# DeltaNet and an MLP mixer in one kernel: 54 steps take another place in the order of issue

## The chip, the cores and the metric

The kernel runs on one core of a Trainium2 chip. A core has a matrix engine (TensorE, PE in the profile, with its weight loads as PEld), a vector engine (DVE), a scalar engine (ACT), GpSimd (POOL) and a queue that issues the transfers between DRAM and on-chip memory (SyncE, SP). Each engine works through its own instructions in the order in which the program issued them, and waits at an instruction until the data and buffers that it needs are there. The metric is the device time of one execution in microseconds (us).

## The reference

Two blocks in a row, all in float32. The first is a DeltaNet attention over 4 batches, 8 heads, 768 positions and a head width of 48:

```
k_n = k / (norm(k) + 1e-6)
for t in range(768):                       # per batch and head
    y[t]  = q[t] @ state                   # state is 48 x 48, from zero
    v_old = state^T k_n[t]
    state = state + beta[t] * outer(k_n[t], v[t] - v_old)
```

The second takes y as x (4 x 768 x 384) and is an MLP mixer, first over tokens, then over channels:

```
h  = relu(x^T @ w_tok1) @ w_tok2           # 768 -> 256 -> 768
u  = x + h^T
out = u + relu(u @ w_ch1) @ w_ch2          # 384 -> 1536 -> 384
```

## The kernel before

**DeltaNet in chunks.** The 768 positions are cut into chunks of 64. Inside a chunk the recurrence is written as matrix products with the inverse of a triangular 64x64 matrix, so that only the step from chunk to chunk is serial. Chunks are handled in units of two (u = 0 to 23). The work on a unit is cut into jobs: `k` loads keys and queries, `p` normalizes and transposes them, `c` (and `d`) make the Gram products, `t` writes the triangular matrices to DRAM (n_dram), `i` inverts a round of several units at once on DVE (x is loaded from n_dram, eliminated row by row on lines 747 and 751, and stored to w_dram), `f` loads the inverses (gm from w_dram), `j` joins parts of an inverse to the whole (p_z and p_x on PE, copies to zst and gm on ACT), `v` loads the values and scales them on POOL. `r0` to `r35` are the serial recurrences. `r24` to `r35` (`recur_pair`) walk through two batches at once: steps 1 to 4 are the p_k products on PE (L1013), step 5 is rw_t on DVE (L1022), steps 6 and 7 are p_y and p_w on PE (L1038, L1042), step 8 is the copy of rw_t on ACT (L1047), steps 9 and 10 are p_s and p_y on PE (L1056, L1059), step 11 updates the state ss_t on DVE (L1070), steps 12 and 13 are ACT's copies of y (L1076, L1081), and step 14 stores one of them to x_dram. The last, `r35`, has no update: its steps 11 to 13 are the two copies and the store.

**The mixer.** `m0` and `m1` (`mixer`) do batches 0 and 1: first the token part (p_h, L1612, with an add of DVE on L1616), then products of the channel part over pieces of 128 rows (p_c, L1672, p_o, L1693) with sums on DVE (L1652) and adds on DVE (L1632). `T2` (`token_part`) is the token part of batch 2: steps 1 to 6 are four matmuls each (L1227), steps 7 to 12 are p_h (L1242) with an add (L1246). `T3`, `S`, `s`, `W` and `A`, `F`, `B` are the token part of batch 3, sums and forms of the weights, and the channel part of batches 2 and 3; `l` loads batch 3 from x_dram.

**The order.** Each job is a Python generator that issues a few instructions between two `yield`s. One long string, written out by hand, names the job whose next step is issued: `m1*4 i4` is four steps of m1 and one of i4. It has 2610 steps.

```python
    for word in order.split():
        name, _, n = word.partition("*")
        for _ in range(int(n or 1)):
            next(jobs[name])
```

The string is the only thing that sets who stands in front of whom on each engine. All transfers are issued on SP. Buffers come from pools that rotate: PSUM, where products land, is divided by tags into 2 buffers for the preparation of units, 2 for the recurrences (`ps_seq`), 3 for the mixer (`ps_mlp`, which the recurrences of pairs borrow from) and one more; a product waits until the reader of what was in its buffer before is done. A transfer also waits for the one eight before it.

Of the kernel before, what the change touches and what calls it, by code (L numbers as in the profile page):

```python
# [23 lines left out]
def kernel(  # L24
# [1756 lines left out]
    w10 p0*2 z w3 w2 c0*3 p0 w3*2 d0*2 w3 c0 p1 c0 d0*3 k2*3 v1 p1*2 w18 k2*2 p1*2  # L1781
    c1*2 d1 k2 p2*2 c1 t0 d1 c1*2 d1*3 t0 p2*8 c2*2 w2 d2 c2*3 Y d2 w2 k3*6 p3
    d2*2 p3 d2 t1*3 x p3*7 c3 k4*5 k7 w13 w18*2 d3*2 v1*2 v0*2 c3*3 v0 c3 d3*3 t0
    p4*2 t2*3 x t3*2 p4*2 x t3 i0*2 w13 p4*2 w18 w17*2 i0 k4 i0*9 p4 i0*2 p4*2 c4
    k8 c4*3 w13*2 w6*2 k5*2 v0 k6 k5*2 i0*2 d4*2 k5 x z d4*3 c4 z*2 p5*2 k5 t4 p5
    h0 h1 h0 w8*2 h1 Y i0 f0 Y p4 f1 h2*2 p5*3 f0*2 w6 h0*5 k6*5 p6 z f2*2 k8*3 p5
    w6 p5 p3 p5 j0*3 f1*2 h1*5 j0*2 w8*2 w17 f2 h2*3 v0 t4*2 w17 r0*5 p6 h2*2 c5*2
    v1 w11*2 j1 p5 k7*2 c5 k7 c5 r0 c5 r0*2 w14*2 v1 w11*2 k7*2 p7 d5*5 r1*5 w14*2
    p6*2 t5 j1 t5*2 r1*2 j1 j2 p7 h3*2 r1*3 p6*3 i1*2 r2*5 k8*2 f3*2 w9 k9*3 j1*2
    v2*2 i1*3 j2*2 r2*2 f3 i1*2 p6*3 w16 v2 w16*3 r2*2 h3 r2 i1 d6 r3*5 i1*2 w9*3  # L1790
    v2 d6 h3 v2 w0 h3*2 r3 h3 d6*2 w0 d6 j3 c6*5 r3*4 w0 j2 w0 p8*2 j2 r4 p8 r4*4
    k9*3 j3*2 r4*2 i1*2 w24 i1*2 p7*7 r4 c7 r4 r5*5 k10 p9 k10 p9 c7 r4 c7*3 i1
    w5*2 p7 r5*2 w24*3 r5*3 j3*2 i1 r6*4 w26 v3*5 p9 k11 r6 d7*5 w26*3 p8*3 t6*2
    r6*2 w5*2 p8*4 v4*2 t6 i1 r6*3 h5*2 h4*2 k10*2 f4*3 c8*2 k10 p10 w28*2 c8*2 r7
    c8 r7*3 d8*4 p9 d8 w28 h4*5 p9 t6 r7*2 j4 w28 p9*3 r7*2 p9 w7 d9 w7 v4*2 f5*2
    w27*2 w7*2 d9*4 c9*2 f5 c9*3 t7*2 t8 r7*2 t7*2 j4*2 v4 p10*2 h5 r8*3 w29 t8*3
    w29 w27*2 r8*2 w29*2 q3 w29 j4*2 r8 w22*4 t9*3 r8*3 p9 r9 p10 r9*3 t9 v5 h5*3
    j5 i2 r9 w4*2 r8 h5 i2*5 w4 i2 w19*2 k10 w32 p10*2 w32 v7 k12 m0*2 k11 k12 q0
    v5*3 p10*2 r9*2 j5*2 k11*3 i2*2 r9 w4 i2 j5 i2*3 p10 v5 r9*2 d10*3 r10 v7*2 j5
    i2*2 r10*4 w12 i2 k12 i2*2 m0 w32 k11 k12 w32 r10*2 m0 p11 k12*4 w19 p11 r10  # L1800
    c10 r10 c10 r10 w33 d10*2 q2 Y r11*4 v7 r11*3 w19 c10 q1 w30 c10 r11 k12*2
    i2*3 r11 v6*4 i2*5 m0*3 i2*5 q5 i2 m0 p11*4 c10 p11 m0 p11*2 m0*2 k12*2 w12
    m0*3 v6 f6*3 w12 d11 c11*2 d11*2 c11 w33 c11 d11*2 j6 p12 w12 m0 w33 w30*3
    p12*2 f7*3 j6*2 m0 c11 j7 f6 f8 w27*2 f8 j7 f8 w15 f7 m0 w29 w33 w29 j7 r12*4
    w31 j8 p11 t10*3 r12 Y r12 f9 j8 f9 w21 p12 r12 f8 r13*2 w15*2 r12 w15 r13*3
    w31*3 Y r13*2 w33 j8 w21 m0 r13 q4 p12*4 r13*2 m0*2 r14 c12 f9 j9 r14*2 w21
    t10 w20*2 v7 r14*2 c12*2 w33 c12 r14 v8 c12*2 r14*2 w25*2 j9 r14 r15 v8 w21
    r14 r15 w25 r15*3 w25 k13*4 w20 k13*4 p13 k13*2 w20 v8*3 m0*2 p13 w25 p13 m0
    r15 p13 r15 p13 w27 w25 k13*2 j9 m0*4 p13 f9 w23 t12*3 p13 t12 w25 r15*3 c13*6
    w23 k14*7 r16*5 m0 p13 m0*3 w23*4 k14 r16*2 t11 t13*2 j9*2 t11*3 w33 p14 r16*2  # L1810
    p14*2 w31 m0*3 w31 m0 w31 m0 w23 r17*2 r16 t13 r17 t13 r17*2 p14*2 m0*2 p14 i3
    k14*4 i3*3 k15 v9*2 m0*3 v10 i3*5 k15 i3 r17 k15*2 p14 k15*3 m0 v10*2 i3 k15*2
    m0*2 k15*2 i3*4 r17*4 k15 i3*2 p14 m0*2 i3*6 m0*4 r18 i3 r18*2 v9*3 r18*2 i3*8
    m0*10 v10*2 m0 r18 c14*4 r18*2 m0*2 f10 c14 f10*2 f12*2 p15*3 m0*4 r18 r19 r18
    r19*3 j10 f10 j10*2 f12 p15 f11*4 f12 r19 c14 r19 v11 p15*3 k16*7 j11 m0*2
    r19*4 j11 j12 r20*3 k16*2 r20 m0 r20 k16*3 v11 m0 j11 r20*2 v11*2 p15 c15*2
    p10 r20*2 c15 r20 c15*3 f13*3 p16 r21*5 m0 r21*2 p16*4 k17*7 p16 j12*2 p16 k17
    r21*3 m0*3 r22 c16 r22*3 k17*4 v11 r22 c16*4 r22*2 m0 r22 t14 p17 f13 c16 t14
    j13*2 t14 r22 r23 t15*2 t16 r23*2 r22 r23 m0*3 r23 t15*2 r23 p17*5 t16 p17 j13
    t16*2 m0*3 t14 c17*5 r23*2 c17 t17*2 m0*8 p17 t17*2 i4*3 v12 m0 k18 v15*2 i4  # L1820
# [14 lines left out]
    f20 m1*3 i6 j18*3 f19 m1*2 S m1 j19*2 j20 j19 f21 r29*2 f21 i6*4 m1*3 i6*6
    j20*2 m1 r30*3 m1*2 r30*2 i6 f21 m1*2 r30 r31*4 r28 r30*2 i6 j21 f20 j21*2
    i6*2 r31*3 v20 i6 v20*2 i6 m1*2 i6*3 r31*4 f21 j21 i6*2 v22*3 v20*2 r32*5 r31
    r29 r31*2 i6*3 m1*5 j21 m1 r32 v21*2 r32 i6*7 m1*2 r30 r32*6 v21*2 s v21 s v22
# [3 lines left out]
    S*3 A0*6 l s l s A0*18 A1 A0*4 A1*2 A0*3 S*3 A0*20 A1*2 T3*2 F0*5 T3*10 A1 S
    T3 A1*3 T3*3 B0 T3*8 B0*3 T3*4 B0 T3 A1*5 T3*3 A1*2 B0*2 A1*6 W A1*3 F0 A1*6
    F0 A1*4 B0 A1*15 A2 F0 A1*3 A2*2 A1*9 F0*2 A1*14 W*3 A2*3 B0*2 A2*5 B0*3 W*2
    F0 B0*3 F1 F0 B0*2 F0*2 B0 A1 B0*4 F0 F1*2 B0*6 A2*10 B1 F1*2 A2*7 B1 A3*2
    A2*3 B0 A2*26 A3 A2*12 F1 A2*2 F1*4 B1*4 A2*5 A3 F1 F2 A3 B1*4 A3*6 F1*2 B1*7
    F1 B1*2 A2 F2*3 F1 B1*6 B2 A3*10 B1*3 A3*15 B1 A3*26 F2*4 A3*3 F2*3 B1 B2*4
    A3*7 B2*5 A3 B2*2 A3*4 F2*2 F3 B2*7 F3*2 B2*2 F3*2 B2 F3*3 B2*6 F3 F2*2 B3*2
# [38 lines left out]
```

## Time and profile before

| | |
|---|---|
| median of 3 runs | 625.38 us (625.58, 625.38, 623.62) |
| profiled execution | 626.48 us |
| its span | 624.7 us |
| mean granted clock of TensorE | 0.973 |
| instructions | 20909 |

The span is the time from the first to the last instruction in the profile, 1.8 us less than the execution's own time. The profile gives for every engine the time in which it was busy and what ended each of its waits. "Issue" as the end of a wait means that nothing in the profile shows what was waited for. In a table of stretches each row has the stretch, its length, the busy time of PE, PEld, DVE, ACT and POOL with the number of their instructions in brackets, the clock granted to TensorE (1.00 is full), the share of time in which the DMA engines were busy, and GB/s. In the chain, a row has start, duration and what it was; in a timeline it also has line, operation, output and inputs with shapes, the number of instructions, and in square brackets the idle time before it and what ended that.

### The profile page before, as it was taken

The page shows a single profiled execution, that of the slowest core. Times are in us where ns is not written, and L with a number is a line of the kernel's source. Part 1 is how long each engine was busy: PE and PEld are TensorE (multiplying, and loading weights), DVE is VectorE, ACT ScalarE, POOL GpSimd, SP SyncE. Part 2 cuts the span into 40 slices and gives each one's busy share as a digit, 9 for nine tenths or more (in the row PEclk, how much of TensorE's full clock was granted, in tenths as well). Part 3 has the DMA queues.
Part 4 walks back from the last instruction along what each step waited for, and adds up shares of the span by engine and source line. Part 5 has one row for each costly group of instructions (what it writes and reads, how often), then busy time and mean ns, then how long its engine had stood idle before and what let it go on. Part 6 is the DMA issues. An engine that isn't in the chain of part 4 may idle for free.

```text
span 624.7 us, 20909 instructions
## 1 busy us (share of the span) xinstructions
PE 594.3 (95%) x8733; PEld 519.7 (83%) x8733; DVE 466.1 (75%) x1160; ACT 256.6 (41%) x682; POOL 110.2 (18%) x150
## 2 busy tenths in 40 slices
...
GB/s 220 125 140 146 143 151 192 137 139 177 129 113 71 64 103 91 102 116 96 104 74 123 93 88 76 35 80 120 32 2 39 1 17 48 14 52 13 14 26 50
DMA packets 154605, 55.52 MB, mean 89 GB/s; under 512 B 129648, under 2 KB 148976, under 8 KB 154512
## 3 DMA queue, kind: packets, MB, share of 16 engines
...
q14 instruction: 25, 0.20, 0.1%
...
## 4 chain that ended last, share of the span: by engine, by line
PE 74%; DVE 10%; DMA 4%; ACT 3%; issue 2%; SPq 2%; POOL 0%; ACTq 0%; DVEq 0%
PE p_c L1672 13%; PE p_r L1502 13%; PE p_o L1693 10%; PE p_a L1574 6%; PE p_b L1574 6%; PE p_g L511 3%; PE p_h L1612 3%; DVE x L751 2%; PE p L1597 2%; DVE sub L747 2%; PE p_k L924 1%; DMA x<-n_dram 1%; PE p_h L1242 1%; PE p_s L962 1%; PE p_y L1038 1%
## 5 line engine op out<-in xcount | busy, mean ns | idle before, releaser
L1672 PE MATMUL p_c<-u_t,wc 128*128 128x256 f32 x432 | 101.6, 386 | 0.6 <-issue 0.6
L1672 PEld LDWEIGHTS p_c<-u_t,wc 128*128 128x128 f32 x432 | 79.6, 190 | 11.9 <-issue 1.1
L1693 PE MATMUL p_o<-wc,r 128*128 128x192 f32 x360 | 64.6, 331 | 0.7 <-DVE xb L1632 0.7
L751 DVE TENSOR_TENSOR x<-x,sub 128x84 f32<-128x84 f32 (+24 forms) x178 | 59.6, 335 | 6.1
L747 DVE TENSOR_TENSOR sub<-x 128x84 f32<-128x84 f32 (+24 forms) x178 | 57.7, 324 | 8.1 <-DMA x<-n_dram 3.5
L1693 PEld LDWEIGHTS p_o<-wc,r 128*128 128x128 f32 x360 | 58.4, 190 | 2.3 <-DVE xb L1632 1.3
L1681 ACT ACTIVATE r<-p_c 128x512 f32<-128x512 f32 x36 | 21.5, 596 | 49.3 <-PE p_c L1672 43.9
L511 PE MATMUL p_g<-kq 48*64 48x128 f32 (+1 forms) x704 | 35.2, 288 | 3.0 <-ACT kq L587 3.0
L517 DVE TENSOR_TENSOR gm<-p_g,mb 128x512 f32<-128x512 f32 x44 | 28.9, 684 | 9.5 <-PE p_g L511 8.4
L484 POOL TENSOR_TENSOR v_st<-v_st,nrm 128x384 f32<-128x384 f32 x12 | 11.2, 931 | 132.4 <-DMA v_st<-in_v_dram 104.8
L511 PEld LDWEIGHTS p_g<-kq 48*64 48x64 f32 (+1 forms) x704 | 27.1, 141 | 7.9 <-ACT kq L587 4.0
L574 POOL TENSOR_TENSOR mb<-mask_c,cs 128x512 f32<-128x512 f32 x20 | 21.2, 1061 | 65.3 <-DVE cs L552 35.7
L293 POOL TENSOR_TENSOR wc<-w_f,d 128x384 uint32<-128x384 uint32 x24 | 24.6, 1030 | 43.3 <-DVE w_f L289 20.2
L1502 PE MATMUL p_r<-t_d,wc 128*128 128x192 f32 x160 | 28.8, 326 | 0.0
L1515 DVE TENSOR_TENSOR kq<-kq,p_r 128x384 f32<-128x384 f32 x40 | 21.1, 552 | 10.2 <-PE p_r L1502 8.3
L1515 DVE TENSOR_TENSOR gm<-gm,p_r 128x384 f32<-128x384 f32 x40 | 21.2, 552 | 8.1 <-PE p_r L1502 5.8
L400 DVE STREAM_TRANSPOSE kq<-pads 128x512 f32<-128x512 f32 x24 | 25.6, 1109 | 1.6 <-DMA pads<-in_k_dram 1.2
L1502 PEld LDWEIGHTS p_r<-t_d,wc 128*128 128x128 f32 x160 | 26.5, 190 | 0.0
L1693 PE MATMUL p_o<-wc,s 128*128 128x192 f32 x144 | 25.7, 330 | 0.7 <-DVE xb L1632 0.7
L1502 PE MATMUL p_r<-pads,wc 128*128 128x192 f32 x128 | 25.4, 326 | 0.0
L1693 PEld LDWEIGHTS p_o<-wc,s 128*128 128x128 f32 x144 | 23.3, 190 | 1.3 <-DVE xb L1632 1.0
L1632 DVE TENSOR_TENSOR xb<-xb,p_o 128x192 f32<-128x192 f32 x42 | 14.7, 349 | 12.7 <-PE p_o L1693 12.3
(315 smaller groups left out, 1390.6 us busy)
## 6 DMA issues: line engine op xcount, KB each, us to landing
...
```

The lines of the kernel that those rows point to most:

```text
L293: nc.gpsimd.tensor_tensor(out=dst.bitcast(U32), in0=f, in1=lo, op=ALU.add)
L400: nc.vector.transpose(kq_of[p // 2][:, i, :, p % 2].rearrange("f p (s g) -> f p g s", g=G), rows_of[i].rearrange("s p (g d) -> s p g d", g ...
L511: nc.tensor.matmul(p_g[PAR[i ^ cc ^ swap(u)], p], kqt[f, p, cc, 0], kqt[f, p, cc])
L517: nc.vector.tensor_tensor(out=blocks(gm_of(u))[:, :, cc, D:GW].rearrange("s p (two n) -> s p two n", two=2), in0=p_g, in1=made[u][:, :, cc ...
L747: nc.vector.tensor_tensor(out=tmp, in0=by[0].to_broadcast(list(to.shape)), in1=by[1].to_broadcast(list(to.shape)), op=ALU.mult,)
L751: nc.vector.tensor_tensor(out=to, in0=to, in1=tmp, op=ALU.add)
L1502: nc.tensor.matmul(p[:, i], pieces[q // width][:, at : at + 128], f[f"u{n}"], start=first and i == 0, stop=True, skip_group_check=True,)
L1515: nc.vector.tensor_tensor(out=o, in0=o, in1=p, op=op_of(sign))
L1574: nc.tensor.matmul(p, a[:, i], w[:, i // 2, i % 2], start=first and i == 0, stop=True, skip_group_check=True,)
L1672: nc.tensor.matmul(p_c[:, k], piece_of(wc1, cb, f * 128)[:, f * 128 : (f + 1) * 128], u_t[:, cb], start=(cb == 0), stop=(cb == NCB - 1),)
L1681: nc.scalar.activation(r2[:, m], p_c, ACTF.Relu)
L1693: nc.tensor.matmul(p, a[:, m], wc2[:, m, j], start=(start and i == 0), stop=(i == NM - 1), skip_group_check=True,)
```

## The change

Only the string differs. Its first 1457 steps are the same, about 280 us of the execution; behind them 54 steps take another place, and all others keep their order. The instructions are the same. The steps that move, with the number of the step of its job:

| stretch of the execution | moved |
|---|---|
| 280 to 300 us | p18's steps 6 and 7 in front of m1's step 7 and i4's last; m1's step 7 behind them; c18's steps 1 to 4 and 6 and p18's step 8 in between r25's steps 8 to 13 |
| 315 to 335 us | t18's steps 1 and 2 sooner, its step 4 and v17's step 1 later (behind t20, and behind t21, right in front of i5); v17's steps 2 to 5 later; m1's step 30 in front of r28's step 6; m1's step 40 in front of i5's step 2 |
| 335 to 375 us | p22's steps 1 to 7 later among i5, m1, v17 and k22; r29's step 5 and i5's step 17 later; m1's steps 51 to 53 from behind i5's last step to in front of r29's step 7; p22's step 8 behind f20's first |
| 400 us | m1's step 87 from behind i6's step 25 to in front of r32 |
| 410 to 445 us | j22's step 1 in front of f23's steps 2 and 3; f23's step 4 from behind r33's step 12 to in front of m1's last; j22's steps 2 and 3 around r33's step 8; T2's step 1 from behind j23's step 2 to behind j22's step 2; v23's step 1 behind r33's step 11; T2's step 2 from behind r33's step 12 to in between r34's step 4 and j23's step 4; T2's step 3 (with r32's step 14) from behind r34's step 8 to behind r34's step 12; r34's step 14 from behind T2's step 9 to in front of r35; T2's step 4 from behind r35's step 8 to behind r35's step 5; T3's step 1 and W's step 5 in front of r35's step 9; r35's steps 11 and 12 behind the loads l |
| 450 to 530 us | S's steps 5 and 8 sooner (28 steps and 37 steps); T3's steps 3 to 5 in front of A0's last step; B1's step 1 two steps of A2 sooner |

The lines of the string with the largest moves, old and new (the string is wrapped anew from its third line on, so that most of the other lines differ by their breaks alone):

```diff
-    p18 k19*8 i4 m1 r25 i4 m1*4 i4 m1 v14 i4*2 v14 i4*8 r24*3 r25*2 m1 v14 i4*2
-    v14*2 p18*2 r25 m1*2 p19 m1*5 k19*4 p19 f14*2 r25*5 c18*5 f14 c18 p18 r26*3
...
-    m1*2 v16 r28 t18 v17 p21*5 t19*4 t18*2 j17 t18 j17 m1*2 r28*3 c21*6 m1*3 r28*3
-    m1*2 r28 m1 t20 s t20*3 t21*4 i5 m1*4 i5 v17*2 r26 i5*2 m1*2 r28 k22*3 i5*4
...
-    i5*2 v19 m1*7 v19 m1*5 r29 c22*5 r29 r27 c22 m1*2 p23*3 m1*3 p23*5 v18 r29 p22
...
-    m1*4 v22 s f22 f23 f22*3 r33*5 f23*2 j22 m1*4 r33*3 v23 j22 r33*2 j22 W j23*2
-    T2 r33*2 T2 f23 r33 l s l s r33 j23 r34*4 j23 r34*2 W*3 v23*4 j23 r34*2 T2 r32
-    r34*5 r35*8 T2 r35*2 T3 W r35*2 l*2 T3 s*5 W*2 T2*5 s r34 r35 A0*7 T2*3 A0*11
...
+    m1*4 i4 m1 v14 i4*2 v14 i4*8 r24*3 r25*2 v14 p18 i4 p18 i4 m1 v14*2 r25 m1*2
+    p19 m1*5 k19*4 p19 f14*2 c18 r25*2 c18 r25 c18 r25 p18 c18 r25 c18*2 f14
...
+    k21 p21 k21 m1*2 v16 r28 t18 p21*5 t19*4 t18 j17*2 m1*3 r28*3 c21*6 m1*2
+    r28*3 m1*2 r28 m1 t20 s t20*3 t18 t21*4 v17 i5 m1*5 i5 r26 i5*2 m1 r28 k22
...
+    p22 i5*3 k23*4 m1*3 r29*2 k23 i5 k23 v18*2 i5*2 v19 m1*4 v19 m1*5 r29 c22*5
...
+    f22*3 r33*5 j22 f23*2 m1*3 f23 m1 r33*2 j22 T2 r33 j22 r33*2 W j23*2 r33 v23
+    r33*2 l s l s r33 j23 r34*4 T2 j23 r34*2 W*3 v23*4 j23 r34*6 T2 r32 r34*2
+    r35*5 T2 r35*3 T3 W r35*2 l*2 r35 T3 r35 s*5 W*2 T2*5 s r35 A0*7 T2*3 A0*11
```

More of the change, by code (lines that the diff above doesn't have):

```diff
@@ L1780 @@
     w10 x*4 z w10*2 z w1*4 k1*3 z k1*3 z b p1 z p1 k0*6 p0*2 b*2 p1 w2 p0*5 p1*2
[L1781 to L1820, printed above, removed]
@@ L1821 @@
-    m0 i4 m0 i4*3 m0 i4 k18*2 j13 p16 m0*2 j13 i4*4 m0 v12*3 k18*4 v12 k18 r24*2
-    r23 v13*5 m0 k18*4 v15*2 i4*2 m0*2 p18 i4 p18 r24*3 m0 r24 i4 m0 p18*2 r25*4
-    p18 k19*8 i4 m1 r25 i4 m1*4 i4 m1 v14 i4*2 v14 i4*8 r24*3 r25*2 m1 v14 i4*2
-    v14*2 p18*2 r25 m1*2 p19 m1*5 k19*4 p19 f14*2 r25*5 c18*5 f14 c18 p18 r26*3
-    p19*2 j14 p19*3 r26*2 f15*4 f14 m1*2 j14 m1 j14 j15*3 s*2 f17*2 m1 f17 m1
-    f16*3 p19 f16 k20*8 j16*3 j17 m1 r26*3 p20 m1*2 p20 r26*2 c19*2 r26 c19 v15
-    r27*2 v16*2 r27*2 p20*2 k20*2 p20 c19*2 r26*2 k20 v16*2 r25 c19 m1*2 f17 r27*4
@@ L1828 @@
-    p20 k20 p20 j17*2 m1 r27*5 c20*4 p20 r28*4 c20*2 k21*9 p21*2 k21*2 p21 k21
-    m1*2 v16 r28 t18 v17 p21*5 t19*4 t18*2 j17 t18 j17 m1*2 r28*3 c21*6 m1*3 r28*3
-    m1*2 r28 m1 t20 s t20*3 t21*4 i5 m1*4 i5 v17*2 r26 i5*2 m1*2 r28 k22*3 i5*4
-    k22*6 m1*2 i5*2 m1*3 i5 v17 r29 i5*3 p22*2 i5 r29 v17 r29*3 i5*2 v19 p22*3
-    k22*3 m1*4 r29 v19*2 i5 k23*6 p22 v18 p22 i5*11 k23*4 r29*2 k23 i5 k23 v18*2
-    i5*2 v19 m1*7 v19 m1*5 r29 c22*5 r29 r27 c22 m1*2 p23*3 m1*3 p23*5 v18 r29 p22
-    f18 m1*3 c23*3 f20*2 f18 c23 f18*2 c23 f19*3 v18 r30 t22*4 c23 t23 r30*4 t23*3
@@ L1835 @@
[L1835 to L1838, printed above, removed]
-    m1*4 v22 s f22 f23 f22*3 r33*5 f23*2 j22 m1*4 r33*3 v23 j22 r33*2 j22 W j23*2
-    T2 r33*2 T2 f23 r33 l s l s r33 j23 r34*4 j23 r34*2 W*3 v23*4 j23 r34*2 T2 r32
-    r34*5 r35*8 T2 r35*2 T3 W r35*2 l*2 T3 s*5 W*2 T2*5 s r34 r35 A0*7 T2*3 A0*11
@@ L1842 @@
[L1842 to L1848, printed above, removed]
@@ L1849 @@
-    F3 B3*10 F3 B2*2 B3*5 F3*4 B3*13
+    w10 p0*2 z w3 w2 c0*3 p0 w3*2 d0*2 w3 c0 p1 c0 d0*3 k2*3 v1 p1*2 w18 k2*2
+    p1*2 c1*2 d1 k2 p2*2 c1 t0 d1 c1*2 d1*3 t0 p2*8 c2*2 w2 d2 c2*3 Y d2 w2 k3*6
+    p3 d2*2 p3 d2 t1*3 x p3*7 c3 k4*5 k7 w13 w18*2 d3*2 v1*2 v0*2 c3*3 v0 c3 d3*3
+    t0 p4*2 t2*3 x t3*2 p4*2 x t3 i0*2 w13 p4*2 w18 w17*2 i0 k4 i0*9 p4 i0*2 p4*2
+    c4 k8 c4*3 w13*2 w6*2 k5*2 v0 k6 k5*2 i0*2 d4*2 k5 x z d4*3 c4 z*2 p5*2 k5 t4
+    p5 h0 h1 h0 w8*2 h1 Y i0 f0 Y p4 f1 h2*2 p5*3 f0*2 w6 h0*5 k6*5 p6 z f2*2
@@ new lines @@
+    k8*3 p5 w6 p5 p3 p5 j0*3 f1*2 h1*5 j0*2 w8*2 w17 f2 h2*3 v0 t4*2 w17 r0*5 p6
+    h2*2 c5*2 v1 w11*2 j1 p5 k7*2 c5 k7 c5 r0 c5 r0*2 w14*2 v1 w11*2 k7*2 p7 d5*5
+    r1*5 w14*2 p6*2 t5 j1 t5*2 r1*2 j1 j2 p7 h3*2 r1*3 p6*3 i1*2 r2*5 k8*2 f3*2
+    w9 k9*3 j1*2 v2*2 i1*3 j2*2 r2*2 f3 i1*2 p6*3 w16 v2 w16*3 r2*2 h3 r2 i1 d6
+    r3*5 i1*2 w9*3 v2 d6 h3 v2 w0 h3*2 r3 h3 d6*2 w0 d6 j3 c6*5 r3*4 w0 j2 w0
+    p8*2 j2 r4 p8 r4*4 k9*3 j3*2 r4*2 i1*2 w24 i1*2 p7*7 r4 c7 r4 r5*5 k10 p9 k10
+    p9 c7 r4 c7*3 i1 w5*2 p7 r5*2 w24*3 r5*3 j3*2 i1 r6*4 w26 v3*5 p9 k11 r6 d7*5
@@ new lines @@
+    w26*3 p8*3 t6*2 r6*2 w5*2 p8*4 v4*2 t6 i1 r6*3 h5*2 h4*2 k10*2 f4*3 c8*2 k10
+    p10 w28*2 c8*2 r7 c8 r7*3 d8*4 p9 d8 w28 h4*5 p9 t6 r7*2 j4 w28 p9*3 r7*2 p9
+    w7 d9 w7 v4*2 f5*2 w27*2 w7*2 d9*4 c9*2 f5 c9*3 t7*2 t8 r7*2 t7*2 j4*2 v4
+    p10*2 h5 r8*3 w29 t8*3 w29 w27*2 r8*2 w29*2 q3 w29 j4*2 r8 w22*4 t9*3 r8*3 p9
+    r9 p10 r9*3 t9 v5 h5*3 j5 i2 r9 w4*2 r8 h5 i2*5 w4 i2 w19*2 k10 w32 p10*2 w32
+    v7 k12 m0*2 k11 k12 q0 v5*3 p10*2 r9*2 j5*2 k11*3 i2*2 r9 w4 i2 j5 i2*3 p10
+    v5 r9*2 d10*3 r10 v7*2 j5 i2*2 r10*4 w12 i2 k12 i2*2 m0 w32 k11 k12 w32 r10*2
@@ new lines @@
+    m0 p11 k12*4 w19 p11 r10 c10 r10 c10 r10 w33 d10*2 q2 Y r11*4 v7 r11*3 w19
+    c10 q1 w30 c10 r11 k12*2 i2*3 r11 v6*4 i2*5 m0*3 i2*5 q5 i2 m0 p11*4 c10 p11
+    m0 p11*2 m0*2 k12*2 w12 m0*3 v6 f6*3 w12 d11 c11*2 d11*2 c11 w33 c11 d11*2 j6
+    p12 w12 m0 w33 w30*3 p12*2 f7*3 j6*2 m0 c11 j7 f6 f8 w27*2 f8 j7 f8 w15 f7 m0
+    w29 w33 w29 j7 r12*4 w31 j8 p11 t10*3 r12 Y r12 f9 j8 f9 w21 p12 r12 f8 r13*2
+    w15*2 r12 w15 r13*3 w31*3 Y r13*2 w33 j8 w21 m0 r13 q4 p12*4 r13*2 m0*2 r14
+    c12 f9 j9 r14*2 w21 t10 w20*2 v7 r14*2 c12*2 w33 c12 r14 v8 c12*2 r14*2 w25*2
@@ new lines @@
+    j9 r14 r15 v8 w21 r14 r15 w25 r15*3 w25 k13*4 w20 k13*4 p13 k13*2 w20 v8*3
+    m0*2 p13 w25 p13 m0 r15 p13 r15 p13 w27 w25 k13*2 j9 m0*4 p13 f9 w23 t12*3
+    p13 t12 w25 r15*3 c13*6 w23 k14*7 r16*5 m0 p13 m0*3 w23*4 k14 r16*2 t11 t13*2
+    j9*2 t11*3 w33 p14 r16*2 p14*2 w31 m0*3 w31 m0 w31 m0 w23 r17*2 r16 t13 r17
+    t13 r17*2 p14*2 m0*2 p14 i3 k14*4 i3*3 k15 v9*2 m0*3 v10 i3*5 k15 i3 r17
+    k15*2 p14 k15*3 m0 v10*2 i3 k15*2 m0*2 k15*2 i3*4 r17*4 k15 i3*2 p14 m0*2
+    i3*6 m0*4 r18 i3 r18*2 v9*3 r18*2 i3*8 m0*10 v10*2 m0 r18 c14*4 r18*2 m0*2
@@ new lines @@
+    f10 c14 f10*2 f12*2 p15*3 m0*4 r18 r19 r18 r19*3 j10 f10 j10*2 f12 p15 f11*4
+    f12 r19 c14 r19 v11 p15*3 k16*7 j11 m0*2 r19*4 j11 j12 r20*3 k16*2 r20 m0 r20
+    k16*3 v11 m0 j11 r20*2 v11*2 p15 c15*2 p10 r20*2 c15 r20 c15*3 f13*3 p16
+    r21*5 m0 r21*2 p16*4 k17*7 p16 j12*2 p16 k17 r21*3 m0*3 r22 c16 r22*3 k17*4
+    v11 r22 c16*4 r22*2 m0 r22 t14 p17 f13 c16 t14 j13*2 t14 r22 r23 t15*2 t16
+    r23*2 r22 r23 m0*3 r23 t15*2 r23 p17*5 t16 p17 j13 t16*2 m0*3 t14 c17*5 r23*2
+    c17 t17*2 m0*8 p17 t17*2 i4*3 v12 m0 k18 v15*2 i4 m0 i4 m0 i4*3 m0 i4 k18*2
@@ new lines @@
+    j13 p16 m0*2 j13 i4*4 m0 v12*3 k18*4 v12 k18 r24*2 r23 v13*5 m0 k18*4 v15*2
+    i4*2 m0*2 p18 i4 p18 r24*3 m0 r24 i4 m0 p18*2 r25*4 p18 k19*8 i4 m1 r25 i4
+    m1*4 i4 m1 v14 i4*2 v14 i4*8 r24*3 r25*2 v14 p18 i4 p18 i4 m1 v14*2 r25 m1*2
+    p19 m1*5 k19*4 p19 f14*2 c18 r25*2 c18 r25 c18 r25 p18 c18 r25 c18*2 f14
+    r26*3 p19*2 j14 p19*3 r26*2 f15*4 f14 m1*2 j14 m1 j14 j15*3 s*2 f17*2 m1 f17
+    m1 f16*3 p19 f16 k20*8 j16*3 j17 m1 r26*3 p20 m1*2 p20 r26*2 c19*2 r26 c19
+    v15 r27*2 v16*2 r27*2 p20*2 k20*2 p20 c19*2 r26*2 k20 v16*2 r25 c19 m1*2 f17
@@ new lines @@
+    r27*4 p20 k20 p20 j17*2 m1 r27*5 c20*4 p20 r28*4 c20*2 k21*9 p21*2 k21 t18
+    k21 p21 k21 m1*2 v16 r28 t18 p21*5 t19*4 t18 j17*2 m1*3 r28*3 c21*6 m1*2
+    r28*3 m1*2 r28 m1 t20 s t20*3 t18 t21*4 v17 i5 m1*5 i5 r26 i5*2 m1 r28 k22
+    v17 k22*2 v17 i5*4 k22*6 m1*2 i5*2 m1*3 i5 r29 i5*3 v17 i5 r29*3 i5 v19 p22
+    v17 k22*2 p22 k22 m1*3 r29 m1 r29 v19*2 i5*2 p22*3 k23*6 v18 i5*6 p22 i5*2
+    p22 i5*3 k23*4 m1*3 r29*2 k23 i5 k23 v18*2 i5*2 v19 m1*4 v19 m1*5 r29 c22*5
+    r29 r27 c22 m1*2 p23*3 m1*3 p23*5 v18 r29 f18 m1*3 c23*3 f20 p22 f20 f18 c23
```

13 lines of the change are left out of this document (added).

## The prediction, made before the changed kernel was run

> **What bounds the kernel now.** I read the page's busy times first, then what PE waits for behind the first moved step (280 us to 482 us), then the table of stretches, and last the chain and the single rows of the stretches that the change touches. The profiled execution took 626.48 us, 1.1 us above the median of the runs (625.38); the sum is made on the profiled one and 1.1 us is taken off at the end.
>
> ```profile
> PE 594.3 (95%) x8733; PEld 519.7 (83%) x8733; DVE 466.1 (75%) x1160; ACT 256.6 (41%) x682; POOL 110.2 (18%) x150
> ```
>
> ```profile
> PE p_o L1693 <- DVE xb L1632: 1.2, 2, 0.7
> PE p_c L1672 <- issue: 0.6, 1, 0.6
> PE p_w L1042 <- DVE rw_t L1022: 0.5, 1, 0.5
> PE p_s L1056 <- issue: 0.4, 1, 0.4
> PE p_k L1013 <- DVE ss_t L1070: 0.2, 1, 0.2
> PE p_h L1376 <- DVE xb L1300: 0.2, 1, 0.2
> ```
>
> PE sets the time: it is busy for 95% of the span, and in the 200 us where the moved steps lie it waits 3.1 us in all. So waits alone can bring little. What else there is to win shows in the granted clock, the last but two of the columns:
>
> ```profile
> 101.30:111.50 10.20, 8.96 (x90) 6.18 (x87) 5.97 (x22) 5.71 (x17) 4.40 (x6) 0.50 0.77 221
> 114.90:118.30 3.40, 2.43 (x47) 1.86 (x40) 3.19 (x9) 1.47 (x5) 0.00 (x0) 1.00 0.61 124
> 118.30:121.80 3.50, 3.50 (x79) 2.09 (x79) 3.33 (x11) 0.74 (x2) 0.20 (x1) 1.00 0.87 186
> 418.41:429.00 10.59, 10.50 (x365) 7.89 (x364) 6.00 (x12) 6.05 (x20) 0.90 (x1) 1.00 0.72 204
> 429.00:432.40 3.40, 2.48 (x99) 1.95 (x98) 0.86 (x4) 1.30 (x4) 0.70 (x1) 1.00 0.04 10
> 432.40:439.20 6.80, 6.53 (x99) 4.66 (x100) 6.66 (x15) 1.12 (x3) 0.00 (x0) 0.50 0.07 17
> 450.00:480.00 30.00, 30.00 (x183) 29.38 (x182) 25.93 (x59) 13.58 (x30) 0.00 (x0) 1.00 0.09 14
> ```
>
> Behind a stretch of 3.4 us in which PE is busy for 2.48 us (73%), mostly with matmuls of 64x64, PE runs 6.8 us at half clock. Behind 450 us it has no gap, so a microsecond won before that is a microsecond at the end.
>
> **The change part by part.** No instruction is added or removed; only who stands ahead of whom on each engine, SP and POOL included, is different.
>
> **The last three recurrences (418 us to 440 us): T2's first four steps, j22, f23, r34, r35.** Their rows:
>
> ```profile
> 429.55 0.43 issue
> ...
> 431.08 0.35 DVE ss_t L1070
> 431.43 0.04 issue
> 431.47 0.61 PE p_k L1013 x24
> ...
> 434.62 2.86 PE p L1227 x4
> 437.48 1.50 PE p_y L1059 x32
> ```
>
> ```profile
> 418.48 0.18 PE p_y L1038
> ...
> 419.56 0.65 PE p_z L855 x32
> ```
>
> ```profile
> 421.97 2.85 PE L1227 MATMUL p<-xb,w 128*128 128x384 f32 x8
> 424.74 0.90 PE L1013 MATMUL p_k<-ss_t,kq 48*64 48x48 f32 x32
> 425.58 0.85 PE L888 MATMUL p_x<-gm,zst 32*32 32x32 f32 x32
> ```
>
> At full clock and with nothing to wait for, the blocks take: r's p_y with p_w 1.08 us (418.48 to 419.56); j22's p_z 0.65; r's p_s with p_y, and j23's p_z, together 1.76 (420.21, where p_z ends, to 421.97), of which about 1.07 and 0.69; the p_k of a recurrence 0.61; one step of T2 1.39 (421.97 to 424.74 for two); j23's p_x 0.65 (an estimate: as the p_z with the same 32 matmuls of 32x32); the last p_y 0.75, half of the 1.50 that it took at half clock. In the new order the PE work from 418.41 up to T2's sixth step is 1.08 + 0.65 + 1.39 + 1.07 + 0.69 + 0.61 + 1.39 + 0.65 + 1.08 + 1.07 + 1.39 + 0.61 + 1.39 + 1.08 + 0.75 + 1.39 = 16.3 us. Before, that stretch lasts from 418.41 to 440.43, which is 22.0 us.
>
> Three waits stand in the new order, and their length is read from ACT:
>
> ```profile
> 419.68 0.48 ACT L1047 COPY rw_t<-p_w 128x384 f32<-128x384 f32 x1 [6.35 <-PE p_w L1042]
> 420.23 0.75 ACT L873 COPY zst<-p_z 32x256 f32<-32x256 f32 x2
> 421.01 0.66 ACT L1076 ACTIVATE xb<-p_y 64x192 f32<-64x192 f32 x2
> 421.68 0.66 ACT L1081 ACTIVATE pads<-p_y 64x192 f32<-64x192 f32 x2
> 422.36 1.06 ACT L866 COPY zst<-p_z 32x128 f32<-32x128 f32 x4
> 423.43 1.07 ACT L869 COPY gm<-p_z 32x128 f32<-32x128 f32 x4
> ```
>
> First, j23's p_x needs the eight copies L866 and L869, behind L1076 and L1081. Those four end 3.5 us after L1076 begins; with T2's first step now in front of r33's p_s, L1076 begins at about 3.9 us after 418.41 and the copies end at 7.4, while PE is there at 6.9: 0.5 us. Before, the same p_x waited for f23's last DMA, issued behind the loads of W and v23; it is now issued in front of m1's last store, some 3 us sooner, and is no longer what ends last. Second and third, r34's p_s and r35's p_y now follow directly on their p_w and wait for the copy L1047 (0.48, and 0.1 around it): 0.6 each. T2's third and fourth steps no longer cover these; they cover the update of ss_t (L1070) and the rw_t of r35 (L1022) instead, which before ended PE waits at 431.47 and 432.67. Sum: 16.3 + 1.7 = 18.0 us against 22.0, a gain of **4.0 us**. About 3.1 us of that is the half clock: T2's fourth step took 2.86 for 1.39, the last p_y 1.50 for 0.75, and the p_w before it about 0.8 too long. So 0.9 us is shorter waiting, and 3.1 hang on the clock staying whole.
>
> Does it stay? The idle of the new order is 0.5 + 0.6 in the stretch from about 425 to 428.5, some 1.1 to 1.3 of 3.4 us, and the rest of that stretch has one or two of T2's steps (128x128 over 384 columns) in it. By busy time that is like the stretch that lost the clock (2.48 us); but 114.90:118.30 is also 2.43 us busy and kept it, with half as many matmuls (47 for 99), so larger ones. I take it that the clock stays, at two to one. The ends are 5.7 us (no wait at all) and 0.9 us (half clock as before).
>
> The Trainium skill, page "TensorE: Matmul & The Clock Gate", section "Why this matters for your kernels", asks for no idle gap over about 3 us to keep the clock. By that rule neither order would drop to half here, and the gain would be the 4.0 us without a doubt; the trace disagrees, since its longest single gap ahead of 432.40 is 0.43 us and the clock fell. The measurement decides, so the doubt stays.
>
> What is queued behind: on SP, r34's store of x_dram moves ahead of two l loads of xb.
>
> ```profile
> 426.21 1.07 SPq L1095 DMA_DIRECT2D xb<-x_dram  x2
> ```
>
> ```profile
> 434.60 0.35 DVE L1300 TENSOR_TENSOR x<-xb 128x192 f32<-128x192 f32 x1
> ...
> 443.41 0.56 DVE L1246 TENSOR_TENSOR xb<-xb,p_h 128x384 f32<-128x384 f32 x1 [3.07 <-PE p_h L1242]
> ```
>
> The store waits for r34's L1081, which ends at about 430 in the new order, so these loads leave 4 to 5 us later than at 426.21, and T3's second step (434.60 before, with s, W and T2's adds queued behind it on DVE) can't come sooner than before. DVE had 3.07 us to spare at T2's first add. PE now comes there 4.0 sooner, so the add is 1 to 1.4 us late; it is caught up within T2's three products, for PE takes 1.3 us for each and DVE 0.56. I cost it at nothing; if the loads are 2 us later still, it costs about 1.3 us.
>
> **The front (283 us to 287 us): p18, m1's step 7.**
>
> ```profile
> 283.26 0.55 DVE L1616 TENSOR_TENSOR xb<-xb,p_h 128x384 f32<-128x384 f32 x1
> ...
> 284.14 1.10 DVE L400 STREAM_TRANSPOSE kq<-pads 128x512 f32<-128x512 f32 x1
> ```
>
> The add at 283.26 goes behind the i4 step (0.44) and the transpose (1.10) and ends at about 285.4 for 283.8. Its PSUM buffer is one of three, and the third product after it wants it at about 284.9: PE waits **0.5 us**. Bounds: 0 (if that product stands 0.5 later than I read it) and 0.6. The i4 store is issued some 0.7 us later; nothing waits for it then. c18 and r25 are woven into each other with the same PE work; I cost this at nothing, within 0.2 either way.
>
> **318 us to 400 us: t18, v17, m1's 30, 40, 51 to 53, p22, r29, i5.**
>
> ```profile
> 334.18 0.19 DVE L747 TENSOR_TENSOR sub<-x 128x30 f32<-128x30 f32 x1 [2.21 <-DMA x<-n_dram]
> ```
>
> m1's add of step 40, which ended the gap of 0.5 us in p_o (two gaps, 1.2 in sum, the longer 0.7), now stands in front of i5's first elimination instead of inside it, so this gap goes. t18's last DMA and the v17 load no longer stand in front of t20's and t21's on SP, so these leave sooner, and the load of x behind them up to 1.5 us sooner; but DVE now waits for step 40's product first, so i5 starts only about 0.6 us sooner, on a DVE that has hardly a pause from 334 to 369. The 0.7 gap keeps its place relative to it. Gain **0.6 us**, bounds 0 and 1.2. Against it: m1's step 51 (three DVE operations, 1.56 us) goes ahead of i5's last three, so i5's result, f18 to f21 and i6 come up to 1.1 us later. Between 380 and 400 us DVE waits twice:
>
> ```profile
> DVE ss_t L1070 <- PE p_y L1059: 1.0, 1, 1.0
> DVE s L1652 <- ACT r L1681: 0.8, 1, 0.8
> ```
>
> That covers it. With the cover gone it would cost the 1.1.
>
> **The rest.** S's step 8 leaves the DVE chain ahead of the 0.2 us gap in p_h L1376: gain **0.2**. m1's step 87, T3's steps 3 to 5, S's step 5 and B1's first product change neighbours on a PE that is full (30.00 of 30.00): nothing, within 0.3.
>
> Sum: 4.0 - 0.5 + 0.6 + 0.2 = 4.3 us, so 622.2 for the profiled execution and **621.1 us** by the median.
>
> **The rivals.** *The half clock comes back* for two stretches of 3.4 us. For it: the busy share of the thin stretch is no better than before. Against it: the matmuls there are larger. Then 0.9 us is left of the 4.0, 1.2 in all: 624.2 us. *It comes back and lasts longer* (slower): it begins one stretch sooner, behind the wait for j23's copies, and holds over T2's steps, as it held 10.2 us from 101.30 on although PE was busy for 8.96. Three stretches cost up to 5.1 us, for 3.1 before: 2.0 lost less 1.2 won, 626.2; four cost 6.8: 3.7 less 1.2, 627.9. It decides from the fourth stretch on; nothing in the stretch behind 429 is as thin as that. *The last loads come too late* and PE waits for T2's adds: 4.3 - 1.3 leaves 3.0, 622.4. *The shorter waits are not worth anything*, since PE was full already: then the clock would not have fallen, and the rows of 434.62 and 437.48 speak against that.
>
> **How the numbers follow.** About 0.3% (1.9 us, so 623.5 and 627.3) is what a measurement of this kernel can tell from no change. Forecast 0.62 (0.60 faster, 0.02 within); half clock as before 0.18 (0.16 within, 0.02 slower with the front's 0.5 and the 1.1 added); half clock longer 0.10 (0.08 slower, 0.02 within); late loads 0.10 (0.08 faster, 0.02 slower with the i5 chain). That gives 0.68, 0.20 and 0.12. The range goes from 619.2 (5.7 - 0.5 + 0.6 + 0.2, and the 0.2 of c18) to 625.0 (the half clock back, and the front's 0.5 not regained); the likeliest case's own is 619.2 to 622.8.
>
> **What would show it.** In the profile after: full clock from 425 to 440; T2's fourth step at about 1.4 us for 2.86; waits of about 0.6 us of p_s and p_y on the copy L1047 and one of p_x on L869, and none on L1070 or L1022; a wait of about 0.5 us of p_h L1612 on the add L1616; one p_o wait for two; DVE waiting for the load of xb ahead of T3's second step. The prediction is wrong if the clock is 0.5 anywhere behind 420, or if p_ut or p_h waits for L1246.

## The result, and the profile after

The changed kernel is slower: the ratio of its runs to those of the kernel before is 1.0063, with a 95% interval from 1.0035 to 1.0090. Its median is 626.51 us over 15 runs (624.06 to 630.21), beside 623.62 us over 15 runs of the kernel before, three of which are the ones shown above. Forecast were 621.1 us, a gain of about 4 us; it lost about 3 to 4.

The profiled execution took 629.22 us, with a span of 626.4 us. The waits of PE behind 278 us, in the columns engine, line and what was waited for, us in all, times, longest:

```profile
PE p_k L1013 <- issue: 2.5, 1, 2.5
PE p_s L1056 <- ACT rw_t L1047: 0.7, 1, 0.7
PE p_y L1059 <- ACT rw_t L1047: 0.6, 1, 0.6
PE p_c L1672 <- issue: 0.3, 1, 0.3
PE p_o L1693 <- DVE xb L1632: 0.3, 1, 0.3
```

Three of them are as the prediction has them: the two waits on the copy of rw_t and one gap in p_o for two, with nothing on L1070 or L1022; p_c waits on "issue" in the trace of before too. The first is in no part of the prediction. It ends with "issue": PE waited for nothing that the profile shows. The chain from 423 us on (start, us, what) shows where it is:

```profile
425.11 0.49 PE p_k L1013 x22
425.60 2.46 issue
428.06 0.43 PE p_k L1013 x10
428.49 1.96 PE p L1227 x4
430.45 0.58 PE p_x L888 x32
```

PE stops inside r34's p_k, after 22 of its 32 matmuls, and goes on 2.46 us later. The stretches around it, in the order PE, PEld, DVE, ACT, POOL, granted clock, DMA share, GB/s:

```profile
425.60:429.40 3.80, 1.34 (x13) 0.98 (x14) 1.31 (x4) 1.86 (x8) 0.00 (x0) 1.00 0.60 157
429.40:432.80 3.40, 3.40 (x98) 2.32 (x96) 3.07 (x3) 1.02 (x4) 1.39 (x1) 0.50 0.17 39
432.80:442.37 9.57, 8.23 (x211) 5.71 (x205) 5.89 (x14) 3.57 (x10) 0.00 (x0) 1.00 0.19 55
```

With PE busy for 1.34 of 3.80 us, the clock falls to half for the next 3.4 us. The whole stretch, from the first of r33's p_y to T2's sixth step, takes this, and in a second trace of the same kernel:

```profile
420.09:442.37 22.28, 18.48 (x566) 13.39 (x565) 12.75 (x28) 9.15 (x29) 1.39 (x1) 0.92 0.39 107
```

```profile
418.46:441.62 23.16, 18.78 (x565) 13.28 (x565) 13.12 (x28) 9.14 (x29) 0.84 (x1) 0.93 0.37 103
```

Forecast for it were 18.0 us; 18.0, the wait of 2.5 and the 1.7 us that 3.4 us at half clock cost make 22.2, so the first row is accounted for. Beside it stand three traces of the kernel before: the one of the prediction, 22.0 us, and two more (the runs e8 and e12 below). The row of e8:

```profile
415.67:434.32 18.65, 17.68 (x566) 13.06 (x565) 12.18 (x27) 9.12 (x29) 0.83 (x1) 1.00 0.46 127
```

Full clock, 18.65 us; e12 has 18.65 too. So the old order took under 19 us here in two of three traces, and the new one 22 to 23 in both.

Times of single executions differ by 6 to 8 us in the runs above, and much of this lies ahead of the change: the first of m1's p_h begins at 276.4 to 283.4 us in the traces of kernels that are the same up to there, with half clock for 20 to 31 us of the first 130. So the stretches of the traces are compared here rather than single times.

### The profile page after: what moved, and what is told of

It reads as the page before. It is cut to its first block, busy times and chain, and to the rows that moved or that the text cites. A ratio compares the mean times of both kernels' runs of the same rounds, so it can differ in the third digit from the quotient of the medians.

```text
span 626.4 us, 20909 instructions
## 1 busy us (share of the span) xinstructions
PE 593.0 (95%) x8733; PEld 517.6 (83%) x8733; DVE 467.9 (75%) x1160; ACT 257.1 (41%) x682; POOL 110.2 (18%) x150
## 4 chain that ended last, share of the span: by engine, by line
PE 74%; DVE 14%; ACT 5%; issue 3%; DMA 2%; SPq 1%; POOL 0%; DVEq 0%; ACTq 0%; POOLq 0%
PE p_c L1672 13%; PE p_r L1502 13%; PE p_o L1693 10%; PE p_a L1574 7%; PE p_b L1574 6%; DVE sub L747 4%; DVE x L751 4%; PE p_g L511 3%; PE p_h L1612 2%; PE p_h L1242 1%; PE p_warm L235 1%; PE p_y L1038 1%; PE p L1227 1%; PE p_h L1376 1%; PE p_s L962 1%
## 5 line engine op out<-in xcount | busy, mean ns | idle before, releaser
L747 DVE TENSOR_TENSOR sub<-x 128x84 f32<-128x84 f32 (+24 forms) x178 | 59.1, 332 | 5.4 <-DMA x<-n_dram 0.7
```

The costliest lines, as they stand in the source:

```text
L747: nc.vector.tensor_tensor(out=tmp, in0=by[0].to_broadcast(list(to.shape)), in1=by[1].to_broadcast(list(to.shape)), op=ALU.mult,)
```

## The experiments

All are orders of the same steps; only e5 adds some. "Stretch" is the one above, from r33's first p_y to the start of T2's sixth step. Each ratio is to runs of the kernel before that were taken beside it. The theory under test stands in e1's expectation: PE's own program is fetched in blocks, and one of them comes late.

**e1: the moves between 410 and 445 us alone, and e2: all others alone.**

```diff
  e1: the old string up to r33*5, then
+ j22 f23*2 m1*3 f23 m1 r33*2 j22 T2 ... W*2 T2*5 s r35
  then the old one; e2: the new string, with the old piece
- r33*5 f23*2 j22 m1*4 r33*3 v23 j22 r33*2 j22 W j23*2 T2 r33*2 T2 f23 ... T2*5 s r34 r35
  in this place
```

> The order of before, with the moves between 410 us and 445 us alone. Theory (late instructions): PE's program comes in blocks of 16 KB; the block that PE needs inside r34's p_k is fetched late, because the DMA engines are full with the loads of W and l, and T2's second step no longer gives it time; so PE waits 2 to 3 us there, with 'issue' as what ended it, and the time is 2 to 4 us above before. Rival (the front moves cost the time): within 0.1% of before. Rival (a buffer or a result that r34's p_k waits for): 2 to 3 us as well, but named in the waits.

> The changed order, with the moves between 410 us and 445 us undone: what is left are the moves before and behind. Theory (late instructions): no wait in r34's p_k; the time is that of before, or up to 0.7 us less (0.5 lost at 285 us, 0.9 won by 340 us, 0.3 at 480 us). Rival (the front moves cost the time): 3 us above before.

e1: 627.16 us, 1.0038 (0.9998 to 1.0078) of before; stretch 22.3 us. e2: 623.02 us, 0.9986 (0.9954 to 1.0019); stretch 18.0 us at full clock. The waits of PE in e1, and then the row of e2's stretch:

```profile
PE p_k L1013 <- issue: 3.0, 2, 2.5
...
PE p_s L1056 <- ACT rw_t L1047: 0.7, 1, 0.7
PE p_y L1059 <- ACT rw_t L1047: 0.6, 1, 0.6
```

```profile
416.63:434.61 17.98, 17.27 (x565) 12.87 (x565) 12.10 (x28) 9.14 (x29) 1.23 (x1) 1.00 0.50 133
```

The moves of the stretch carry the loss: e1's interval just takes in no change, but its stretch is that of the changed kernel, with the same wait in r34's p_k (2.5 us of the 3.0; the other 0.4 stands at 397 us). The others are within the measurement of no change; that they cost 3 us falls.

**e3: T2's second step back in front of r34.**

```diff
- r33*2 l s l s r33 j23 r34*4 T2 j23
+ r33*2 l s l s r33 j23 T2 r34*4 j23
```

> The changed order, with T2's second step alone put back in front of r34's first. Theory (late instructions): its eight slow matmuls give the fetch 1.4 us more, so the wait in r34's p_k falls from 2.5 us to 1 us or nothing; 1.5 us or more below the changed kernel. Rival (a result or a buffer): the wait moves with r34 and stays about 1 us or is gone too; this run alone does not tell these apart.

626.49 us, 1.0043 (1.0011 to 1.0075); stretch 23.1 us. A miss in time:

```profile
PE p_s L1056 <- issue: 1.2, 1, 1.2
PE p_k L1013 <- issue: 1.0, 1, 1.0
```

The wait in p_k falls from 2.5 to 1.0, about the length of a step of T2, as expected (the step has four matmuls, not the eight that the expectation names); but the next block of 256 instructions is late in its turn, in r34's p_s, where T2's second step now no longer stands ahead of it. The half clock lasted 6.8 us here.

**e4: the load of W sooner.**

```diff
- f22*3 r33*5 j22 f23*2 m1*3 f23 m1 r33*2 j22 T2 r33 j22 r33*2 W j23*2
+ f22*3 r33*5 W j22 f23*2 m1*3 f23 m1 r33*2 j22 T2 r33 j22 r33*2 j23*2
```

> The changed order, with the load of W (576 KB) alone issued some 5 us sooner, in front of j22's first step. Theory (late instructions): the DMA engines are free when PE's block is asked for at about 422 us, the block comes 1 to 3 us sooner and the wait in r34's p_k shrinks to under 1 us; some 2 us below the changed kernel. Rival (a result or a buffer): nothing that r34's p_k reads has moved, so the wait stays 2.5 us.

624.80 us, 1.0019 (0.9976 to 1.0062); stretch 20.8 us.

```profile
PE p_k L1013 <- issue: 0.9, 1, 0.9
```

No operand of p_k has moved, nor any instruction of PE, and the wait falls from 2.5 to 0.9 us. That speaks for the late block, and against a result or a buffer.

**e5: the borders of the blocks moved.**

```diff
- c2*3 Y d2
+ c2*3 Y*13 d2
```

> The changed order, with 12 more steps of warm tiles (48 matmuls of 64x64, some 190 instructions of PE) in the first 50 us, where PE has idle time. Nothing else moves, but every later border between two blocks of PE's program now falls 190 instructions sooner in the work. Theory (late instructions): the wait of 2.5 us with 'issue' in r34's p_k goes, or shrinks to under 1 us and stands in another product. Rival (a result or a buffer that r34's p_k waits for): it stays at 2.5 us in the same place. The time itself tells less, since the extra matmuls move the clock of the first 130 us too.

630.74 us, 1.0114 (1.0073 to 1.0156), most of it ahead of 290 us and not of use; stretch 20.2 us at full clock. The waits of PE behind 278 us:

```profile
PE p_z L847 <- issue: 1.8, 1, 1.8
PE p_s L1056 <- issue: 0.8, 1, 0.8
PE p_s L1056 <- ACT rw_t L1047: 0.7, 1, 0.7
PE p_y L1059 <- ACT rw_t L1047: 0.6, 1, 0.6
PE p_x L888 <- issue: 0.4, 1, 0.4
```

In r34's p_k there is no wait at all; in the stretch p_s and p_x have one instead (0.8 and 0.4). The 1.8 us of p_z stand at 321 us, where the changed kernel's trace has no wait on "issue", and half clock for 3.4 us follows them there. The wait goes with the count of instructions, not with the work. This is the clearest of the runs on this point.

**e6: the loads of W and of l out of the way.**

```diff
- ... r33*2 W j23*2 r33 v23 r33*2 l s l s r33 ... W*3 v23*4 j23
+ r33*5 W j22 ... r33*2 j23*2 r33 v23 r33*2 s*2 r33 ... W*3 v23*3 l*2 v23 j23
```

> The changed order, with the load of W (576 KB) in front of j22's first step and the first two loads l (192 KB each) behind v23's last. Theory (late instructions): with both out of the way of PE's block, no wait in r34's p_k is above 0.5 us; the stretch from the first of r33's p_y to T2's sixth step, 22.2 us in the changed kernel, takes the 18.0 us of the prediction where the clock stays full, and up to 20 where a stretch of 3.4 us falls to half; the time is 2 to 4 us below the changed kernel and 0 to 2 us below before. Rival (the half clock alone, whatever the wait): 21 to 22 us as before.

625.48 us, 0.9996 (0.9964 to 1.0028); the wait is 1.1 us and the stretch 19.6 us, with the clock whole:

```profile
PE p_k L1013 <- issue: 1.1, 1, 1.1
```

```profile
419.98:439.58 19.60, 17.18 (x565) 12.59 (x565) 12.05 (x28) 9.14 (x29) 0.84 (x1) 1.00 0.45 122
```

Half of what was expected: moving the l loads as well (they stand in front of v23's last step) takes off nothing more than W's load alone did in e4, and 1.1 us of the wait stays. But the loss of the change is not seen any more, and without its wait the stretch would take 18.5 us, near the 18.0 of the prediction.

**e7: the old order of the stretch, with W and f23's last in front.**

```diff
- f22*3 r33*5 f23*2 j22 m1*4 r33*3 v23 j22 r33*2 j22 W j23*2 T2 r33*2 T2 f23 r33
+ f22*3 r33*5 W f23*2 j22 m1*3 f23 m1 r33*3 v23 j22 r33*2 j22 j23*2 T2 r33*2 T2 r33
```

> The moves of the change before 410 us and behind 450 us, the old order between them, but the load of W in front of f23's second step and f23's last in front of m1's last. Theory: the late block of PE costs the old order less, since T2's first two steps stand together in front of r34; with the loads out of the way its 'issue' waits (0.4 us in p_s) and the wait for f23 (0.5 us) go as well; 0.5 to 1.5 us below the run with the front moves alone, 1 to 2 us below before. Rival (the loads are hidden in the old order): the same as the front moves alone.

624.76 us, 1.0008 (0.9975 to 1.0040); stretch 19.0 us. No gain: j23's p_z waits now.

```profile
PE p_z L847 <- DMA out_dram<-xb: 0.9, 1, 0.9
```

```profile
418.18 0.45 DVE L817 STREAM_TRANSPOSE t<-gm 128x256 f32<-128x256 f32 x1 [2.31 <-DMA gm<-w_dram]
```

The profile names a store, which landed at about the same time; but p_z reads t, and begins at 418.67, right behind the transposition that makes t. That one waited 2.31 us for f23's loads of gm, which stand behind W's load here.

**e9: the first half of the stretch in the old order, and e10: the second half.**

```diff
  e9: the new string with
- r33*5 j22 f23*2 m1*3 f23 m1 r33*2 j22 T2 r33 j22 r33*2 W j23*2 r33 v23 r33*2 l s l s r33 j23 r34*4 T2 j23
+ r33*5 f23*2 j22 m1*4 r33*3 v23 j22 r33*2 j22 W j23*2 T2 r33*2 T2 f23 r33 l s l s r33 j23 r34*4 j23
  e10: the new string with
- r34*6 T2 r32 r34*2 r35*5 T2 r35*3 T3 W r35*2 l*2 r35 T3 r35 s*5 W*2 T2*5 s r35
+ r34*2 T2 r32 r34*5 r35*8 T2 r35*2 T3 W r35*2 l*2 T3 s*5 W*2 T2*5 s r34 r35
```

> The changed order, with the moves of j22, f23, v23 and T2's first two steps undone, and those of T2's third and fourth steps, r34 and r35 kept. Theory (late instructions): T2's first two steps lie together in front of r34 again and give the fetch 2.8 us, so there is no 'issue' wait over 0.5 us in r34's p_k; the waits on the copy L1047 (0.7 and 0.6) stay. The stretch from m1's last p_o to T2's sixth step takes 18 to 19.5 us at full clock. Rival (the two waits on L1047 cost the time): 2 us above the old order's 18.2 to 18.9.

> The changed order, with the moves of T2's third and fourth steps, r34 and r35 undone, and those of j22, f23, v23 and T2's first two steps kept. Theory (late instructions): the wait of about 2.5 us in r34's p_k stays, and the clock falls behind it; the same stretch takes 21 to 23 us. Rival (the two waits on L1047 cost the time): 18 to 19.5 us.

e9: 624.09 us, 1.0018 (0.9987 to 1.0050); stretch 18.7 us, full clock, with no wait on "issue" in it. Its waits and, behind them, the first of e10:

```profile
PE p_s L1056 <- ACT rw_t L1047: 0.7, 1, 0.7
PE p_y L1059 <- ACT rw_t L1047: 0.6, 1, 0.6
PE p_x L888 <- DMA gm<-w_dram: 0.3, 1, 0.3
```

```profile
PE p_k L1013 <- issue: 2.5, 1, 2.5
```

e10: 629.72 us, 1.0094 (1.0061 to 1.0127); stretch 22.0 us, half clock for 3.4 us. So the loss sits in the first half of the stretch. e9 puts j22, f23 and v23 back together with T2's first two steps, so it doesn't tell these apart; the counting below speaks for T2's steps. The waits on L1047 are in e9 too and cost nothing against the waits that they replace: 18.7 us for the old 18.65.

**e8 and e12: the kernel before, and e11: the changed kernel, for more traces.**

> The kernel before once more, for a second trace of its stretch from 418 us to 440 us. If the half clock of 6.8 us found there belongs to the order, it is there again, and the stretch takes 22 us; if it hangs on where the stretch of 3.4 us begins, the order can also take some 18 us, as it did in the run with the front moves alone, and then the prediction counted 3 to 4 us to be won that most executions don't lose.

> The changed kernel once more, for a second trace. If the wait in r34's p_k belongs to the order, it is there again at 2 to 3 us, and the stretch takes 20.5 us or more; if the first trace met it by chance, it takes 18 to 19 us.

> The kernel before once more, for a third trace of the same stretch: 18.2 to 19 us at full clock, or some 22 us with half clock; the two traces so far have one of each.

e8 (622.43 us) and e12 (624.62 us) have full clock behind 280 us and a stretch of 18.65 us each. e11 (628.67 us) has the wait again, and the clock falls behind it:

```profile
PE p_k L1013 <- issue: 3.1, 1, 3.1
```

**How late the block is.** The page's third part lists a queue of its own for instructions, q8, with packets of 16 KB: 68 in the kernel before, for some 17,600 records of PE (matmuls and weight loads together), so one for about 259. If blocks of 256 instructions are what PE waits for, its waits on "issue" must stand 256 records apart, and they do: in the fourteen traces there are 74 waits of PE over 0.15 us that end with "issue" (counted from the traces), and each of them is in front of a record 194 or 195 past a multiple of 256. In e5, whose steps stand 192 records later, they are in front of the same records and so of other work. The wait in r34's p_k is in front of record 14787, e3's second wait in front of 15043, and the 0.43 us in the prediction's trace in front of 15042. In the 49 of these waits that lie behind 130 us, PE goes on 2.2 to 2.9 us after a packet of q8 begins. No rival that was named, a result or a buffer, would keep to such a count.

Behind 450 us, where PE takes few and long instructions and the DMA engines are mostly idle, the packet of each block begins when PE is 159 to 198 instructions past a multiple of 256. In the stretch, the one that is due at record 14787 begins this far past 14336, a multiple of 256:

| kernel | instructions past it | what PE waited at record 14787 |
|---|---|---|
| changed, e11, e10 | 449, 449, 449 | 2.5, 3.1, 2.5 us |
| e1, e3 | 423, 410 | 2.5, 1.0 |
| e4, e6 (W's load sooner) | 273, 276 | 0.9, 1.1 |
| e9 | 388 | none |
| before, e8, e12 | 402, 271, 267 | none |
| e2, e7 | 310, 267 | none |

At 449 PE stands still or is about to, so a packet that is later still shows no larger number. In the changed kernel's trace there is no packet of q8 between 418.50 and 425.50; the transfers of that time and, in the next tenth of a microsecond, its start (packets, MB, share of the time of 16 DMA engines):

```profile
q1 hardware_dynamic: 2352, 1.16, 61.3%
issues: line engine op xcount, KB each, median us to landing
wc<-wc_dram SPq DMA_DIRECT2D x1, 576.0 KB, 4.4
out_dram<-xb SPq DMA_DIRECT2D x2, 192.0 KB, 1.9
xb<-x_dram SPq DMA_DIRECT2D x2, 192.0 KB, 4.6
```

```profile
q1 hardware_dynamic: 73, 0.03, 113.3%
q8 instruction: 1, 0.02, 67.2%
```

The packet begins at 425.53, and PE goes on at 428.06, 2.5 us later; it was 2.5 us in e11 and 2.9 in e1. An estimate of when the block is called for: some 165 instructions past the multiple, as the packet of the block just ahead of the stretch (164 to 176 past it), so at PE's record 14501, and it is needed at 14787. In the order before, T2's first two steps (2.8 us with only 8 matmuls and 8 weight loads) are records 14733 and on, between the two, and PE takes 4.8 us from the one to the other (420.4 to 425.2). In the changed order T2's first step is at 14477, just ahead of the call, and its second at 14809, just behind the point where the block is needed; what is left in between is small matmuls, 2.2 us (423.4 to 425.6). A block that needs 2.5 us from its packet on can't come in time for that, even if the packet isn't late. It was 2.1 us late in the changed kernel and 0.8 in e6 (423.3 to 424.1), where 0.8 + 2.5 - 2.2 = 1.1 is the 1.1 us that PE waited. In the prediction's trace of the order before it was 2.4 us late (420.4 to 422.8), and PE did not wait there: T2's two steps covered it. So by these counts the place of the two steps is what the change lost, and the lateness adds to it.

One thing more differs. In the changed order T2's first step delays the call itself, from 2.0 to 3.3 us into the stretch, while W's load is issued at 0.9 to 2.2 us in either: the call comes 1.1 to 2.4 us behind that load in the five traces with this step in its new place (changed, e1, e3, e10, e11), and at most 0.4 behind it in the five with the old place (before, e2, e8, e9, e12). The packet is 1.8 to 2.8 us late in the first five, and 0.9 to 1.4, once 2.4, in the others. That may be why; no run separates it.

The Trainium skill, page "Runtime: NRT & Kernel Launch", section "Instruction fetch mechanics", says that an engine's program is refilled in blocks of 16 KiB, 256 instructions, through a DMA queue of its own, and that crossing into the next block is mostly hidden. The size agrees with the 68 packets and the 256 between the waits here; the hiding does not hold in this stretch, where it cost 2.5 us.

## Why the prediction was wrong

*The sum of the stretch.* 16.3 us of PE work and 1.7 us of waits. The step that failed is the list of waits: it names three, each on a result, and the largest in the changed kernel, 2.5 us on PE's own program, is not among them. The trace of before did show its kind, as the 0.43 us of "issue" in r34's p_s and the 0.6 us in p_c; the prediction prints both rows, and its sum for the new order has no such wait, without a cause given for them. Of the three that were named, the two on L1047 came as forecast (0.7 and 0.6 for 0.6 each); the one on the copies of j23 (0.5) is hidden behind the long one. Where the long one is short, the sum is near: 18.5 us in e6, without its 1.1 us.

*The clock.* "I take it that the clock stays, at two to one" failed as well, but not for the reason weighed there. The stretch from 425 us on was to have 1.1 to 1.3 us of idle; it had 2.46 in one piece, and the clock fell in both traces of the kernel, and in e1, e3, e4 and e10, but in the stretch not in e5, e6 and e9. The limit of about 3 us that the prediction took from the Trainium skill (page "TensorE: Matmul & The Clock Gate", section "Why this matters for your kernels") was not reached in the profiled execution, nor in e4, where the longest wait was 0.9 us, and yet the clock fell, as in the trace of before; in e11 the wait was 3.05 us.

*What could be won.* 3.1 of the 4.0 us were the half clock of the profiled execution. In two more traces of the same order it isn't there, nor in e2, which has the old order here: these take 18.0 to 18.7 us. So even a new order that takes 18.0 us would have won 0.7 us against the 18.65. The mistake was to take one execution's half clock for a property of the order. Against 18.65 us, the changed kernel's 22.3 and 23.2 lose 3.6 and 4.5 us, which is about what the times show.

*The rivals.* That the half clock comes back was on the list at 0.18, priced as no change since the old order was taken to have it too. That it lasts longer, the case that was to end slower, did not happen: it lasted 3.4 us. None of the rivals names a wait on instructions.

*The front.* Forecast a loss of 0.5 us; from the first of m1's p_h to its last it takes 7.52 us in the four traces with the old front and 7.92 to 8.02 in the ten with the new one, so 0.4. The add now follows the transpose, as forecast, and ends at 287.3:

```profile
285.75 1.10 DVE L400 STREAM_TRANSPOSE kq<-pads 128x512 f32<-128x512 f32 x1
286.75 0.54 DVE L1616 TENSOR_TENSOR xb<-xb,p_h 128x384 f32<-128x384 f32 x1
```

*318 to 400 us.* Forecast a gain of 0.6 us, with one p_o gap gone: the gap went (0.3 us in one gap for 1.2 in two; the old order has 1.0 in two and 0.5 in one in its other traces). From the first of m1's p_h to its last p_o the new front takes 136.8 to 137.6 us and the old 136.2 to 137.2 (e1, with a wait on keys elsewhere, and e5, with that at 321 us, left out), so of a gain nothing is left with the front's 0.4 in it.

*The last loads.* They left at 436.38 for 426.21, 8.5 us later in the stretch where 4 to 5 were forecast; in e9, without the long wait, it is 4.9. T2's first add still waits for PE, by 0.20 us for 3.07, and by as much in e6 and e9. Costed at nothing, rightly.

```profile
445.35 0.55 DVE L1246 TENSOR_TENSOR xb<-xb,p_h 128x384 f32<-128x384 f32 x1 [0.20 <-PE p_h L1242]
```

*S's step 8.* Forecast 0.2; from T2's last product to the end it takes 173.87 us for 174.15, so 0.3; the other traces with the new place and the old agree with this within 0.02 us.

What stays open: why, in the same order, the block begins 402 instructions past the multiple of 256 in one trace and about 270 in two; which transfers besides W's load delay it (e4 and e6 are one trace each); and what sets the half clock behind it, which cost 1.7 us of the loss: it came behind a wait of 0.9 us in e4 and not behind 1.1 in e6. No order that was tried is shown to be faster than the kernel before; e2, at 0.9986, can't be told from it.
